# Moving the attention of groups five to eleven by a weight pair, holding their first scores, and chunking three more groups' Q and K

## The chip, the cores and the metric

The kernel runs on one NeuronCore of a Trainium2 chip. A core has a matrix engine (TensorE, PE in the profile, with weight loads shown apart as PEld), a vector engine (VectorE, DVE), a scalar engine (ScalarE, ACT), a general engine (GpSimd, POOL) and a queue engine (SyncE, SP) that here issues most DMA transfers. Each engine works through its own instruction stream in order, and they wait for each other by semaphores. The metric is the device time of one execution, in microseconds.

## The reference

Two layers, one behind the other. The first is a linear attention with a complex decay, for 4 batches, 8 heads, 768 steps and 48 channels a head:

```python
a_re_n, a_im_n = (a_re * scale, a_im * scale)      # scale = min(|a|, 0.999) / (|a| + 1e-6)
for t in range(S):
    S_re, S_im = ar * S_re - ai * S_im + k[t] v[t]^T, ar * S_im + ai * S_re
    y[:, :, t] = q[:, :, t] @ S_re
```

The second is a mixture of four dense experts on the 3072 rows of 384 that y makes:

```python
p = domain_probs / (domain_probs.sum(-1, keepdims=True) + 1e-09)
for e in range(E):
    out += p[:, e:e + 1] * (np.maximum(x @ w1[e], 0.0) @ w2[e])   # 384 -> 1024 -> 384
```

Everything is float32 in and out.

## The kernel before, in words

**Groups and blocks.** The 3072 rows are cut into twelve groups of 256 (three to a batch), each of two chunks of 128. While the attention of group g is computed, TensorE also does experts 0 and 1 for the rows of group g-1: that is block g-1. So block 4 carries the attention of group 5. After the last block a second phase does experts 2 and 3 for all rows.

**A block's dense part.** The weights of two experts lie in SBUF as sixteen tiles, taken two at a time: eight weight pairs, k = 0 to 7. For a pair, `w1_step` makes the first layer (tile `ph`, 18 matmuls, line 237: each weight and each x is split in a high and a low part, and three products are summed), ScalarE and VectorE make the hidden rows in high and low part (`hh` line 247, `hl` line 248), and `w2_step` adds the second layer to `po` (line 258, 12 matmuls). The second layer of a pair is emitted after the first layer of the next one.

**Attention of a group.** VectorE and ScalarE prepare it ahead, in `norm` (decays normalised), `prefix` (running products of decays, lines 423 to 426 and 366 to 374) and `finish`, whose head multiplies Q with them (line 494) and whose tail makes K (lines 509 to 513). Q and K are then in a layout with channels of all heads in the partitions. `trip` turns them to one head's channels in the partitions by writing them to DRAM (`q_d`, `k_d`, line 523) and reading them back (`Qst`, `Kst`, line 530). `attention` uses them in three pieces:

- the first: K of chunk 0 turned on TensorE (`ktp`, line 564), the state's increment (`dp`, line 583), and the first scores (`sc`, line 599, two halves of eight matmuls in all, masked on VectorE into `scs`, line 604);
- the second: values of chunk 0 (`yp`, lines 616 and 621), decay factors, scores of chunk 1;
- the third: values of chunk 1, y to DRAM (`y_d`, line 699) and back as the block's next input (`xa`, line 217), the turn and increment of chunk 1, and the state's rotation (lines 639 to 642, not for the last group of a batch; nor are its turn and increment of chunk 1).

The input is split in high and low part (`xha` line 224 on ScalarE, `xla` line 226 on VectorE), emitted ahead of pair 7 and needed at the next block's first pair.

**Where the pieces stand.** `between(k)` is called ahead of each pair of a block. From `FIRST[g]` on (2 where it has no entry) it emits one piece of group g's attention at each of three calls, so the third piece stands ahead of pair `FIRST[g]` + 2. At each call it also advances the preparation of the next group, by a budget in microseconds (`STEP`, `MORE`). One point of that stream is held: the tail of group g+1, which writes K, is emitted only after the third piece of group g's attention (`over`).

**HALF.** For the groups in `HALF`, Q and K make the trip one chunk at a time, and the tail computes K one chunk at a time, chunk 0 first; the others send both chunks in one transfer for each of the real and the imaginary part. After a group's trips stands a tiny DMA that reads `Kst` (line 873), and behind it on SP the loads of the next group's Q and K and of the decays after that.

**Order.** The emission gives the order by which a planner arranges the instructions: it simulates the engines with its own costs and moves instructions ahead of others on the same engine when it believes them ready. `behind(ins, prev)` forbids one such move: `ins` may not be placed ahead of `prev` on the engine, without a wait of its own. The planner's clock is not the chip's, so an instruction can be placed where the chip does not have its data yet.

Of the kernel before, what the change touches and what calls it, by code (L numbers as in the profile page):

```python
# [55 lines left out]
WARM = {6: "pq", 7: "tk"}  # L56
NSEL = 2
XSEL = 3
FIRST = {1: 5, 2: 5, 3: 4, 4: 4, 5: 3, 6: 3}
STEP = {1: 4.2, 2: 4.2, 3: 4.2, 4: 4.2, 5: 4.2}  # L60
MORE = (1.9, 1.9, 0.5)
HALF = (2, 3, 4, 5)
HOFF = 96
WIDE = 32 + P + 48
DMA_SCRATCH = 4096
# [56 lines left out]
def fast_path(ctx, tc, qkP, aP, vP, probsP, w, out, flag):  # L122
# [41 lines left out]
    wts = {}  # L164
    whi = {}

    def behind(ins, prev):
        tc.add_manual_dep(ins.ins, prev.ins.name,
                          mybir.DependencyInfo(mybir.DependencyClass.NoSync, mybir.DependencyReason.DATA),
                          reason="issue order")  # L170
# [44 lines left out]
    def load_x(g):  # L215
        x = moe.tile([P, NJ, G], F32, tag="x", name=f"xa{g}", bufs=1)
        nc.sync.dma_start(x, y_d[g].rearrange("(j p) t -> p j t", p=P))
        return [(slice(0, G), x)]
# [11 lines left out]
    def w1_step(b, xh, xl, f2, prev=None):  # L230
        ph = ps_h.tile([P, 2, G], F32, tag="ph", name=f"ph{b}_{f2}")
        for u in range(2):
            hi, lo = wts[2 * f2 + u]
            n = 0
            for wt, xt in ((hi, xh), (lo, xh), (hi, xl)):
                for j in range(NJ):
                    ins = nc.tensor.matmul(ph[:, u, :], wt[:, j * P:(j + 1) * P], xt[:, j, :],  # L237
                                           start=(n == 0), stop=(n == 3 * NJ - 1))
                    if u == 1 and n == 0:
                        wts["w1"] = ins  # L240
                        tc.keep_in_program_order(ins)
                    elif n == 0 and prev is not None:
                        behind(ins, prev)
                    n += 1
        hh = moe.tile([P, 2, G], F32R, tag="hh", name=f"hh{b}_{f2}")
        hl = moe.tile([P, 2, G], F32R, tag="hl", name=f"hl{b}_{f2}")
        wts["hh"] = nc.scalar.activation(hh, ph, AF.Relu)  # L247
        nc.vector.scalar_tensor_tensor(hl, ph, 0.0, hh, op0=ALU.max, op1=ALU.subtract)  # L248
        return hh, hl
# [16 lines left out]
    class MoE:  # L266
# [8 lines left out]
        def block(self, b, xh, xl, f_lo, f_hi, done, between=None, prev=None):  # L275
            po = None
            for f2 in range(f_lo // 2, f_hi // 2):
                if between is not None:
                    between(f2 - f_lo // 2)
                hh, hl = w1_step(b, xh, xl, f2, prev if f2 == f_lo // 2 else None)  # L280
                self.flush()
                if (2 * f2) % FE == 0:
                    po = [ps_o.tile([P, HD], F32, tag="po", name=f"po{b}_{f2}_{t}") for t in range(CG)]

                def fin(f2=f2, hh=hh, hl=hl, po=po):
                    w2_step(f2, hh, hl, po, wts.pop(("hold", b, f2), ()))
                    if (2 * f2 + 2) % FE == 0:
                        done(2 * f2 // FE, po)
                self.pend = fin
# [3 lines left out]
    with ExitStack() as c1:  # L293
# [225 lines left out]
        def trip(nm, X, dst, lo=0, hi=CG, prev=None):  # L519
            w = X.shape[-1] if hi == CG else C  # L520
            dt = dram.tile([2, HD, hi - lo, w], F32, name=nm)
            for c in range(2):
                sent = nc.sync.dma_start(dt[c].rearrange("(j p) n t -> p j n t", p=P),
                                         X[:, c].rearrange("p (j n) t -> p j n t", n=CG)[:, :, lo:hi, :w])
                if prev is not None:
                    behind(sent, prev)

            def back(prev=None):
                for c in range(2):
                    landed = nc.sync.dma_start(dst[c * IM:c * IM + D, :, lo:hi, :w],  # L530
                                               dt[c].rearrange("(h d) n t -> d h n t", d=D))
                    if prev is not None:
                        behind(landed, prev)
                return landed
            back.sent = sent
            return back

        def t_factors(g):
            Tr, Ti = Qst[0:D, :, CG - 1, C:], Qst[IM:M, :, CG - 1, C:]
            ins = nc.scalar.activation(TA[0:D], Tr, AF.Copy)  # L540
            tc.keep_in_program_order(ins)
            behind(ins, state["y", g, CG - 1 if g < NSEL else 0])
            tc.keep_in_program_order(nc.scalar.activation(TA[IM:M], Tr, AF.Copy))
            tc.keep_in_program_order(nc.scalar.activation(TB[IM:M], Ti, AF.Copy))
            tc.keep_in_program_order(nc.scalar.activation(TB[0:D], Ti, AF.Copy, scale=-1.0))
# [85 lines left out]
        def rotate(g):  # L631
            if (g + 1) % GB == 0:
                return
            Gt = state[g, CG]

            def bt(ap):
                return ap.broadcast_to([ap.shape[0], H, D])

            nc.vector.tensor_tensor(P2[0:D], Gt[IM:M], bt(TB[IM:M]), op=ALU.mult)
            nc.vector.tensor_tensor(P2[IM:M], Gt[0:D], bt(TB[0:D]), op=ALU.mult)  # L640
            nc.vector.tensor_tensor(Gt, Gt, bt(TA), op=ALU.mult)
            state["dve"] = nc.vector.tensor_tensor(Gt, Gt, P2, op=ALU.add)
            state[g + 1, 0] = Gt

        def turn_x(g, c, y):
            xp = ps_a.tile([P, NJ, C], F32, tag="pa", name=f"xp{g}_{c}")
            for j in range(NJ):
                ps = [p for p in range(HP) if -HOFF < 2 * D * p - P * j < P]
                for p in ps:
                    o = HOFF - (2 * D * p - P * j)  # L650
                    ins = nc.tensor.matmul(xp[:, j, :], band[:, o:o + P], y[:, p, c * C:(c + 1) * C],
                                           start=(p == ps[0]), stop=(p == ps[-1]))
                    if g == 0 and c == 0 and p == ps[0]:
                        behind(ins, state["yl", g, 1])
            last["xp"] = ins
            return slice(c * C, (c + 1) * C), xp
# [39 lines left out]
        def store_y(g, y):  # L696
            yv = y_d[g].rearrange("(p u d) t -> u d p t", u=2, d=D)
            for u in range(2):
                nc.sync.dma_start(yv[u], y[u * IM:u * IM + D])

        def attention(g, QK):
            y = small.tile([M, HP, G], F32, tag="y", name=f"y{g}")
            (turn0, _, inc0, sc0, val0), (turn1, _, inc1, sc1, val1) = (chunk(g, c, QK[1], y) for c in range(CG))
            turn0()
            inc0()
            yield sc0()
            val0()
            t_factors(g)
            sc1()
            xs = [turn_x(g, 0, y)] if g < XSEL else None  # L710
            if g < XSEL:
                wts["hold", g - 1, NF1 // 2 - 2] = ((5, state["sc", g, 1]),)
            yield
            val1()
            if g < XSEL:
                xs.append(turn_x(g, 1, y))
                wts["hold", g - 1, NF1 // 2 - 1] = ((0, state["yl", g, 1]), (8, last["xp"]))
            store_y(g, y)
            x = xs or load_x(g)
            turn1()  # L720
            inc1()
            rotate(g)
            yield x
# [67 lines left out]
        def front(g, A, qk):  # L791
# [36 lines left out]
            yield 3.0  # L828
            if g in HALF:
                qb = [trip(f"q_d{g}_{c}", Q, Qst, c, c + 1) for c in range(CG)]  # L830
# [10 lines left out]
            else:  # L841
# [5 lines left out]
                qb()  # L847
                last["q"] = kb()
            todo[g] = attention(g, (Q, K))

        x = {}
# [54 lines left out]
        for g in range(1, NG + 1):  # L906
            if g == NG:
                check_all()
                for e, h in late_d:
                    late_weights(e, h)  # L910
            first = FIRST.get(g, 2)
            end = first + len(MORE) - 1
# [586 lines left out]
```

## Time and profile before

| what | value |
|---|---|
| timed runs | 981.01, 984.24, 989.49 us; median 984.24 |
| the profiled execution | 989.45 us, its span 987.6 us |
| granted TensorE clock, mean | 0.988 of full |
| ScalarE, GpSimd busy | 479.6 us (49%), 165.9 us (17%) |
| DMA | 139.60 MB, mean 141 GB/s |

The profile is one execution. Its page gives busy times, the chain of work that ended last and the costliest groups of instructions; the trace behind it also answers which engine waited for what, in any stretch of time, and lists instructions in order. Lines such as L599 are lines of the kernel, and a name such as `Kst<-k_d` is what an instruction writes and what it reads. Matmuls are pipelined, so a busy TensorE is not always one at its peak. The blocks of attention last from about 51 to 614 us, the second phase from there to the end. Block 4 begins at about 238 us, and blocks 4 to 10, in which groups 5 to 11 have their attention, end at about 573 us.

### The profile page before, as it was taken

How to read it: one execution, taken by the hardware profiler on the slowest of the kernel's cores; microseconds unless marked ns; L12 is line 12 of the kernel's file. 1: busy time of each engine (PE TensorE's matmuls, PEld its weight loads, DVE VectorE, ACT ScalarE, POOL GpSimd, SP SyncE). 2: the span in 40 equal slices, each digit the busy share in tenths (PEclk: the TensorE clock that was granted, in tenths of full speed). 3: DMA queues.
4: the chain of work that ended last, by engine and by line, in shares of the span. 5: the costliest groups of instructions: out<-in, count | busy, mean ns of one | idle time of the engine just before them, and what ended most of it. 6: DMA issues, size and time to landing. Idle time of an engine off the chain costs nothing.

```text
span 987.6 us, 18277 instructions
## 1 busy us (share of the span) xinstructions
PE 952.5 (96%) x7037; PEld 920.5 (93%) x7037; DVE 739.5 (75%) x1610; ACT 479.6 (49%) x952; POOL 165.9 (17%) x206
## 2 busy tenths in 40 slices
PE   5899999999998999999999999999999999999997
PEld 2799999999898989899998999999999999999997
DVE  7889989898787989788887556767575848576643
ACT  7755536354353626264444345645554545454430
POOL 6030000000000000000000006533443342323000
PEclk9899999999899999999999999999999999999999
DMA  9585277582837556483939759421513453231112
GB/s 309 171 163 151 73 177 155 143 194 88 200 96 177 129 153 168 105 192 113 217 90 290 279 167 329 103 97 48 129 55 114 157 138 90 75 97 49 49 49 76
DMA packets 112258, 139.60 MB, mean 141 GB/s; under 512 B 8034, under 2 KB 95890, under 8 KB 112162
## 3 DMA queue, kind: packets, MB, share of 16 engines
q1 hardware_dynamic: 100674, 111.42, 39.7%
q0 software_dynamic: 11488, 26.93, 11.7%
q8 instruction: 57, 0.93, 0.4%
q14 instruction: 39, 0.32, 0.1%
HBM read 89.82 MB, written 48.49 MB: 140 GB/s over the span
## 4 chain that ended last, share of the span: by engine, by line
PE 75%; DMA 12%; DVE 6%; ACT 3%; issue 1%; SPq 0%; DVEq 0%; ACTq 0%
PE pob L961 20%; PE pb L961 17%; PE ph L237 13%; PE po L258 13%; PE sc L599 5%; DMA Kst<-k_d 4%; DMA k_d<-K 4%; PE yp L621 2%; PE yp L616 2%; DMA q_d<-Q 2%; PE dp L583 1%; DVE K L513 1%; DMA y_d<-y 1%; PE ktp L564 1%; DVE Q L494 1%
## 5 line engine op out<-in xcount | busy, mean ns | idle before, releaser
L961 PE MATMUL pob<-shi,hid 128*128 128x384 f32 x528 | 148.4, 334 | 0.0
L258 PE MATMUL po<-whi,hh 128*128 128x384 f32 x384 | 130.5, 340 | 0.0
L258 PE MATMUL po<-wlo,hh 128*128 128x384 f32 x384 | 129.3, 337 | 0.0
L247 ACT ACTIVATE hh<-ph 128x512 fp32r<-128x512 f32 x96 | 57.2, 596 | 111.9 <-PE ph L237 102.9
L973 POOL TENSOR_TENSOR Z<-Z 128x384 f32<-128x384 f32 x84 | 90.7, 1125 | 111.0 <-DMA Z<-y_d 56.2
L237 PE MATMUL ph<-xha,whi 128*128 128x256 f32 x576 | 104.0, 287 | 1.2 <-ACT xha L224 1.2
L237 PE MATMUL ph<-xha,wlo 128*128 128x256 f32 x576 | 102.8, 284 | 0.0
L237 PE MATMUL ph<-xla,whi 128*128 128x256 f32 x576 | 101.6, 284 | 0.6 <-DVE xla L226 0.6
L961 PE MATMUL pb<-xh,shi 128*128 128x384 f32 x291 | 97.2, 335 | 0.6 <-DVE pb L967 0.6
L961 PEld LDWEIGHTS pob<-shi,hid 128*128 128x128 f32 x528 | 96.4, 188 | 0.2 <-DVE hid L970 0.2
L961 PE MATMUL pb<-xh,slo 128*128 128x384 f32 x288 | 96.2, 334 | 0.0
L961 PE MATMUL pb<-xl,shi 128*128 128x384 f32 x288 | 96.2, 334 | 0.0
L248 DVE SCALAR_TENSOR_TENSOR hl<-ph,hh 128x512 fp32r<-128x512 f32 x96 | 65.9, 687 | 38.7 <-ACT hh L247 38.1
L237 PEld LDWEIGHTS ph<-xha,whi 128*128 128x128 f32 x576 | 86.0, 190 | 2.9 <-ACT xha L224 1.7
L961 PE MATMUL pob<-slo,hid 128*128 128x384 f32 x264 | 88.2, 334 | 0.0
L258 PE MATMUL po<-whi,hl 128*128 128x384 f32 x384 | 86.4, 338 | 0.0
L237 PEld LDWEIGHTS ph<-xla,whi 128*128 128x128 f32 x576 | 82.9, 191 | 1.2 <-DVE xla L226 0.8
L237 PEld LDWEIGHTS ph<-xha,wlo 128*128 128x128 f32 x576 | 83.1, 190 | 0.4 <-issue 0.2
L964 ACT ACTIVATE SN<-pb 128x384 f32<-128x384 f32 x96 | 47.3, 492 | 66.6 <-PE pb L961 59.2
L967 DVE TENSOR_TENSOR xl<-Z,xh 128x384 fp32r<-128x384 f32 x104 | 59.8, 606 | 21.1 <-ACT xh L964 10.9
L258 PEld LDWEIGHTS po<-whi,hh 128*128 128x128 f32 x384 | 72.7, 189 | 0.8 <-ACT acc L729 0.2
L258 PEld LDWEIGHTS po<-wlo,hh 128*128 128x128 f32 x384 | 72.8, 190 | 0.0
(227 smaller groups left out, 2050.6 us busy)
## 6 DMA issues: line engine op xcount, KB each, us to landing
qk<-qkP SPq DMA_DIRECT2D x24, 384.0 KB, 5.7
acc_d<-acc POOLq DMA_DIRECT2D x24, 384.0 KB, 5.2
ACC<-acc_d SPq DMA_DIRECT2D x48, 192.0 KB, 3.6
A<-aP SPq DMA_DIRECT2D x22, 384.0 KB, 6.8
Z<-y_d SPq DMA_DIRECT2D x16, 384.0 KB, 3.6
q_d<-Q SPq DMA_DIRECT2D x12, 387.0 KB, 5.0
Qst<-q_d SPq DMA_DIRECT2D x12, 387.0 KB, 5.9
v<-vP SPq DMA_DIRECT2D x24, 192.0 KB, 2.4
```

The source lines that it names most:

```text
L237: ins = nc.tensor.matmul(ph[:, u, :], wt[:, j * P:(j + 1) * P], xt[:, j, :], start=(n == 0), stop=(n == 3 * NJ - 1))
L247: wts["hh"] = nc.scalar.activation(hh, ph, AF.Relu)
L248: nc.vector.scalar_tensor_tensor(hl, ph, 0.0, hh, op0=ALU.max, op1=ALU.subtract)
L258: ins = nc.tensor.matmul(po[t], part[0][:, u, t * P:(t + 1) * P], wts[i][n][:, HD:], start=(i % FE == 0 and part[0] is hh and n == 0), sto ...
L494: ins = nc.vector.tensor_tensor(dst(Q[:, c, :, :C], lo, hi), rows(A[:, c], lo, hi), rows(qk[:, 0], lo, hi), op=ALU.mult)
L599: ins = nc.tensor.matmul(s_ps[:, h, :], Kc[:, hf * 4 + h, :], Qc[:, hf * 4 + h, :], start=True, stop=True)
L616: ins = nc.tensor.matmul(yo, st[:, o:o + n], Qc[:, o // D, :], start=True, stop=False)
L621: ins = nc.tensor.matmul(yo, vc[:, o:o + n], sc[h // 4][:, h % 4, :], start=first, stop=True)
L961: return tc.keep_in_program_order(nc.tensor.matmul(*args, **kw))
L964: return pin(nc.scalar.activation(dst, src, fn, scale=scale))
L967: pin(nc.vector.tensor_tensor(dst, x, y, op=op))
L973: nc.gpsimd.tensor_tensor(dst, x, y, op=op)
```

## The change

Three edits.

- `FIRST` is raised: groups 5 and 6 from 3 to 4, group 7 from 2 to 4, groups 8 to 11 from 2 to 3. All three pieces move together, and with the third piece the point after which the next group's tail is emitted.
- The first scores (both halves of chunk 0) of groups from `NPIN` = 5 on are placed behind the last first-layer matmul that was emitted before them, that of pair `FIRST[g]` - 1. The planner could move them ahead of it until now.
- Groups 6, 7 and 8 join `HALF`.

```diff
-FIRST = {1: 5, 2: 5, 3: 4, 4: 4, 5: 3, 6: 3}
+NPIN = 5
+FIRST = {1: 5, 2: 5, 3: 4, 4: 4, 5: 4, 6: 4, 7: 4, 8: 3, 9: 3, 10: 3, 11: 3}
...
-HALF = (2, 3, 4, 5)
+HALF = (2, 3, 4, 5, 6, 7, 8)
...
                     n += 1
+        wts["w1e"] = ins
         hh = moe.tile([P, 2, G], F32R, tag="hh", name=f"hh{b}_{f2}")
...
             turn0()
             inc0()
-            yield sc0()
+            yield sc0(prev=wts["w1e"] if g >= NPIN else None)
             val0()
```

## The prediction

> **What bounds the kernel now.** I read the page's busy line and chain first, then TensorE's waits (over the span and block by block), then the granted clock by stretch, and last the chain and timelines around groups five, six and seven.
>
> ```profile
> PE 952.5 (96%) x7037; PEld 920.5 (93%) x7037; DVE 739.5 (75%) x1610; ACT 479.6 (49%) x952; POOL 165.9 (17%) x206
> PE 75%; DMA 12%; DVE 6%; ACT 3%; issue 1%; SPq 0%; DVEq 0%; ACTq 0%
> ```
>
> TensorE is busy 96% of the 987.6 us span, yet only 75% of the chain that ended last is TensorE, and 12% is DMA. So some work comes just late, off TensorE. TensorE's waits (engine, line, what ended the wait: total, times, longest) show what:
>
> ```profile
> PE sc L599 <- DMA Kst<-k_d: 11.5, 7, 3.4
> ```
>
> Most of what TensorE waits for in the middle of the kernel is the first scores of a group, for K on its way back from DRAM. The same question put to stretches of about one block each gives, for groups 5, 6, 7, 8, 10 and 11 in this order (group 9 has no such wait):
>
> ```profile
> PE sc L599 <- DMA Kst<-k_d: 2.4, 1, 2.4
> PE sc L599 <- DMA Kst<-k_d: 3.4, 1, 3.4
> PE sc L599 <- DMA Kst<-k_d: 1.3, 1, 1.3
> PE sc L599 <- DMA Kst<-k_d: 1.1, 1, 1.1
> PE sc L599 <- DMA Kst<-k_d: 0.7, 1, 0.7
> PE sc L599 <- DMA Kst<-k_d: 2.1, 1, 2.1
> ```
>
> Sum: 2.4 + 3.4 + 1.3 + 1.1 + 0.7 + 2.1 = 11.0 us, all in groups that the change moves. Now the clock, by stretch (start:end, length, busy us of PE, PEld, DVE, ACT and POOL, granted clock, DMA share, GB/s):
>
> ```profile
> 261.50:268.40 6.90, 6.58 (x50) 6.29 (x51) 2.86 (x8) 0.00 (x0) 0.00 (x0) 0.51 1.12 281
> 312.70:316.10 3.40, 3.40 (x18) 3.40 (x18) 1.20 (x3) 0.00 (x0) 0.00 (x0) 0.51 0.91 355
> 316.10:541.40 225.30, 220.19 (x1928) 209.97 (x1927) 191.06 (x433) 108.22 (x202) 7.15 (x10) 1.00 0.61 158
> 541.40:544.90 3.50, 3.50 (x17) 3.50 (x18) 3.09 (x7) 0.63 (x1) 0.00 (x0) 0.51 1.07 292
> ```
>
> After each of the three waits over 2 us (groups 5, 6, 11) the clock is granted at half for 6.9, 3.4 and 3.5 us; between 316 and 541 us, where the waits are 1.3 us or less, it stays at 1.00. Half clock costs half of those stretches: 0.49 x 13.8 = 6.8 us.
>
> What the change can win in this execution is thus 11.0 + 6.8 = 17.8 us. Three blocks, each read from the second pair's start to the next block's second pair, bear it out:
>
> ```profile
> 242.30:292.30 50.00, 47.53 (x376) 45.42 (x376) 39.43 (x91) 22.15 (x42) 1.43 (x2) 0.93 0.55 135
> 292.30:342.80 50.50, 47.14 (x398) 45.06 (x398) 42.02 (x88) 27.90 (x50) 1.44 (x2) 0.97 0.61 159
> 435.90:481.10 45.20, 45.20 (x398) 43.45 (x397) 38.54 (x84) 23.08 (x43) 1.44 (x2) 1.00 0.59 151
> ```
>
> The block from 435.9 has no wait, TensorE is full, and it lasts 45.2 us; those from 242.3 and 292.3 last 50.0 and 50.5. VectorE needs 38.5 to 42 us of a block of 45: it has room, but only some 3 to 7 us, which matters below.
>
> **Part by part.** *Scores later and held.* A weight pair is one 18-matmul first layer (ph) and one 12-matmul second layer (po):
>
> ```profile
> 338.69 2.15 PE ph L237 x18
> 340.84 2.08 PE po L258 x12
> 312.49 3.53 PE sc L599 x16
> 316.02 0.21 PE ph L237
> 316.24 2.11 PE po L258 x12
> ```
>
> One pair is 2.15 + 2.08 = 4.23 us. What counts is not the move in the emission but how much TensorE work that now stands behind the first scores comes ahead of them. The hold forbids scores before the last first-layer matmul of pair FIRST - 1. For group 6 (the last three rows, in the chain's order) the scores now sit one ph short of a pair's first layer; they go behind that ph and, I expect, the twelve po: 0.21 + 2.11 = 2.3 us against a 3.4 us wait. Group 7, moved by two pairs, and 8 to 11 get between half a pair and a whole one, 2.1 to 4.2 us, against 1.3, 1.1, none, 0.7 and 2.1: covered. Group 5 is different; its scores were late already:
>
> ```profile
> 261.82 0.77 PE sc L599 x2
> 262.59 1.67 PE dp L583 x26
> 264.26 3.29 PE sc L599 x14
> 267.55 1.65 PE po L258 x7
> ```
>
> They stand behind pair 3's first layer, which is just what the hold asks, so only the seven po move ahead (7 x 2.08/12 = 1.2 us at full clock), and perhaps the increment (26 dp, half of 1.67, 0.8 us at full clock). That leaves 2.4 - 1.2 - 0.8 = 0.4, to 1.2 us; I take 0.7. At 1.3 us and less the clock held, by the rows above.
>
> *Q and K by chunk for six to eight.* The DMA issues (out<-in, count, KB each, median us to landing), then the VectorE forms of the K product (count, busy, mean ns, idle before):
>
> ```profile
> k_d<-K SPq DMA_DIRECT2D x12, 384.0 KB, 6.6
> Kst<-k_d SPq DMA_DIRECT2D x12, 384.0 KB, 5.5
> k_d<-K SPq DMA_DIRECT2D x16, 192.0 KB, 3.9
> Kst<-k_d SPq DMA_DIRECT2D x16, 192.0 KB, 5.1
> L513 DVE TENSOR_TENSOR K<-A,u 128x384 f32<-128x384 f32 x24 | 12.1, 550 | 0.1
> L513 DVE TENSOR_TENSOR K<-A,u 128x768 f32<-128x768 f32 x12 | 10.9, 952 | 0.0
> ```
>
> The first chunk's trip is 3.9 + 5.1 = 9.0 us instead of 6.6 + 5.5 = 12.1: 3.1 us earlier, for groups 6 to 8. Against it stand ten half-size VectorE operations for five whole ones, 10 x 0.55 - 5 x 0.95 = 0.75 us a group at most, and eight more DMA issues a group on SP, queued ahead of the next Q/K and A loads, which have most of a block to land. I cost both at nothing: VectorE's 3 to 7 us and SP's idle time hide them; uncovered, the VectorE part is 3 x 0.75 = 2.3 us.
>
> *What is late next: the next block's input.* A group's third piece stores y, reloads it as x and splits it, due when the next block starts; for group 5 it moves one pair nearer to that start. The chain there today, the first matmul of the next block, and two jobs that group 6 has behind its third piece:
>
> ```profile
> 280.21 0.61 ACT y L627
> 280.83 4.57 DMA y_d<-y
> 285.46 2.97 DMA xa<-y_d
> 288.45 0.85 ACT xha L224
> 289.33 0.96 DVE xla L226
> 290.29 0.47 DVE s L489
> 292.29 0.52 PE L237 MATMUL ph<-xha,whi 128*128 128x256 f32 x3
> 327.80 0.81 PE ktp L564 x6
> 333.12 0.95 PE dp L583 x27
> ```
>
> From the start of y's last copy (280.21) to the end of xha (289.30) it is 9.1 us, and the block starts 12.1 us after that copy: 3.0 us to spare. One pair takes 4.23 of it, so x(5) is late by 1.2 us, bounded by 0 (if a second layer is put first) and 3 (a slower DMA). I take 1.4. Groups 6 and 7 also end at pair 6, but have a turn and an increment behind the third piece, 0.81 + 0.95 = 1.8 us more cover: on time. Groups 8 to 11 end at pair 5 and keep a pair.
>
> The row of s L489 shows the other side: VectorE's head work for K(6) stands behind xla(5) today. With x(5) later and the head emitted before it, I expect that order to turn and K(6) to come sooner; if not, K(6) moves with x(5), and group 6 keeps up to 2 us of its wait. I take 0.7.
>
> **Sum.** The profiled execution took 989.45 us (span 987.6). 989.45 - 17.8 + 0.7 (scores of 5) + 1.4 (x of 5) + 0.7 (scores of 6) = 974.5. The three timed runs (981.01 to 989.49, median 984.24) reach below that execution; I read this as fewer or shorter waits of this kind in them, which lowers what can be won there but not the floor of 989.45 - 17.8 = 971.7. Against the median, 974.5 is -1.0%.
>
> **Rivals.** *K moves along (0.22).* The stream emits the next group's K only after this group's third piece, so K(6) to K(11) may come as many pairs later as the scores. For it: the order of emission. Against it: around 290 us the work ahead of K is the chain of x quoted above, not an emission. Then the waits stay, less what the chunks' 3.1 us take: 3.1 + 1.3 + 1.1 and group 6's half clock, 1.7, together 7.2. With 1.4 for x(5): 989.45 - 7.2 + 1.4 = 983.7, the median's level.
>
> *The half clock stays (0.06).* If the three stretches at 0.51 had another cause than the waits before them, only group 6's, behind the longest, would go: 989.45 - 11.0 - 1.7 + 2.8 = 979.6. Against it: each starts as such a wait ends, and between 316 and 541 us there is none. [...]
>
> *The x load takes the place (0.12, slower).* The starts of blocks 5, 6 and 7 wait for x instead. The cover from y's last copy to the next start becomes 12.1 - 4.2 = 7.9 us for group 5 and 9.7 for 6 and 7. If store and load meet the stream's transfers and take what K's whole ones take (6.6 + 5.5, with 0.6 of copy and 0.85 of split 13.6), x is late by 5.7 + 3.9 + 3.9 = 13.5 us, and the clock halves after each (three times 1.7 to 3.4, say 8): 989.45 - 17.8 + 13.5 + 8 + 1.4 = 994.5. It decides from a chain of about 11.7 us, where all three waits pass 2 us and the clock begins to fall (971.7 + 1.4 + 7.8 + 5.1 = 986); today's rows show 9.1, which speaks against it.
>
> *More than counted (0.04).* Below 969, if VectorE, no longer held behind late scores, also closed small gaps elsewhere; no row promises it.
>
> **Numbers.** The forecast case has 0.56, with its own range of 970 to 979. With the second and third cases the range is 969 to 986. About 1% is what a measurement of this kernel can tell from no change: 974.4 and 994.1. Rather over half of the forecast case lies below 974.4, since the waits added are taken high and the runs' spread comes mostly from waits that go; with the last case 0.38 faster. The rest of it, the second and third cases and a part of the fourth make 0.52 the same; 0.10 slower.
>
> **What would show it.** Right: no wait of the first scores for Kst over about 1 us in groups 5 to 11, no half clock between 240 and 600 us, blocks of 44 to 47 us there, a small wait of ph for xha or xla near 288 us. Wrong: waits of scores that stay though their place among the pairs moved (the second case), waits of ph for xha or xla over 3 us at several block starts (the fourth), or half clock without a wait before it (the third).

## The result and the profile after

The changed kernel takes 974.76 us in the median of five runs (973.38 to 975.42), the kernel before beside it 985.34 (981.01 to 989.49): a ratio of 0.9908, interval 0.9881 to 0.9935. (Ratios here are estimates over the runs side by side; the quotient of the two medians is 0.9893.) The forecast was 974.5. The profiled execution took 974.37 us (span 972.7) against 989.45 before: 15.1 us less.

The page of the changed kernel, its busy line, the granted clock in 40 slices and the chain that ended last:

```profile
PE 945.0 (97%) x7037; PEld 913.5 (94%) x7037; DVE 740.7 (76%) x1625; ACT 480.1 (49%) x952; POOL 165.6 (17%) x206
...
PEclk9999999999999999999999999999999999999999
...
PE 84%; DVE 5%; DMA 4%; ACT 2%; issue 1%; SPq 0%; POOL 0%; DVEq 0%; ACTq 0%
```

DMA's share of the chain falls from 12% to 4%, TensorE's rises from 75% to 84%. TensorE's busy time falls by 7.5 us with the same 7037 matmuls. At half clock matmuls last longer and count as busy for longer (before, group 11's first scores took 421 ns each at a granted clock of 0.51, group 9's 275 ns at 1.00, in the median); the forecast's 6.8 us of half clock are most of this. TensorE's waits from 235 to 562 us (engine, line, what ended the wait: total, times, longest) are now these:

```profile
PE sc L601 <- DMA Kst<-k_d: 1.5, 1, 1.5
PE sc L601 <- issue: 1.0, 1, 1.0
PE yp L623 <- DVE scs L606: 0.2, 1, 0.2
PE po L260 <- ACT acc L731: 0.2, 1, 0.2
```

The first is group 11's, the second group 9's; groups 5, 6, 7, 8 and 10 have none. (For some waits no releaser is found and the view says "issue"; group 9's stands where a wait for `Kst` would.) The 11.0 us of before are 2.5.

The seven blocks that carry groups 5 to 11, cut at the same matmuls as before (start:end, length, busy us of PE, PEld, DVE, ACT and POOL, granted clock, DMA share, GB/s):

```profile
242.10:286.80 44.70, 44.53 (x376) 42.55 (x376) 41.27 (x95) 24.13 (x45) 1.43 (x2) 1.00 0.65 163
286.80:331.70 44.90, 44.90 (x398) 43.35 (x398) 38.34 (x87) 23.86 (x44) 1.44 (x2) 1.00 0.67 154
331.70:380.80 49.10, 49.10 (x433) 46.89 (x432) 44.71 (x100) 25.41 (x47) 1.43 (x2) 1.00 0.65 157
380.80:422.10 41.30, 41.30 (x356) 40.02 (x355) 34.79 (x78) 19.75 (x35) 1.43 (x2) 1.00 0.57 149
...
sum 319.40, PE 316.52 PEld 302.74 DVE 267.98 ACT 153.88 POOL 10.02; mean PE 45.22 PEld 43.25 DVE 38.28 ACT 21.98 POOL 1.43
```

The sum of the same view of before:

```profile
sum 334.50, PE 323.56 PEld 309.37 DVE 266.57 ACT 153.44 POOL 10.02; mean PE 46.22 PEld 44.20 DVE 38.08 ACT 21.92 POOL 1.43
```

334.5 - 319.4 = 15.1 us: all of the gain lies in these blocks. The first two fall from 50.0 and 50.5 to 44.7 and 44.9, the length that the undisturbed block of before had (45.2). Single blocks aren't comparable further than that, because some work moved from one to the next (433 matmuls in the third against 414 before, 356 in the fourth against 375); the sums are comparable.

### The profile page after: what moved, and what is told of

Same layout as the page of the kernel before. It is cut to its first block, busy times and chain, and to the rows that moved or that the text cites. A ratio compares the mean times of both kernels' runs of the same rounds, so it can differ in the third digit from the quotient of the medians.

```text
span 972.7 us, 18333 instructions
## 1 busy us (share of the span) xinstructions
PE 945.0 (97%) x7037; PEld 913.5 (94%) x7037; DVE 740.7 (76%) x1625; ACT 480.1 (49%) x952; POOL 165.6 (17%) x206
## 4 chain that ended last, share of the span: by engine, by line
PE 84%; DVE 5%; DMA 4%; ACT 2%; issue 1%; SPq 0%; POOL 0%; DVEq 0%; ACTq 0%
PE pob L963 20%; PE ph L238 18%; PE po L260 17%; PE pb L963 17%; PE sc L601 4%; PE yp L623 2%; PE dp L585 2%; PE yp L618 2%; PE ktp L566 1%; DMA lw<-w 1%; DMA shi<-w 1%; PE xp L653 1%; DMA Kst<-k_d 1%; DVE Q L496 1%; DMA q_d<-Q 1%
## 5 line engine op out<-in xcount | busy, mean ns | idle before, releaser
L966 ACT ACTIVATE hid<-pb 128x384 fp32r<-128x384 f32 x76 | 37.3, 490 | 71.9 <-PE pb L963 71.4
```

What stands on the lines that cost most here:

```text
L966: return pin(nc.scalar.activation(dst, src, fn, scale=scale))
```

## The experiments

Each diff says which kernel it starts from. Line numbers are those of the changed kernel, two higher than before. `NPIN`, and the line that notes the last first-layer matmul, do nothing by themselves.

**The parts alone.** Four kernels compared on one chip with the kernel before (983.55 us in the median of 29 runs). First, only `FIRST`; against the changed kernel:

```diff
-HALF = (2, 3, 4, 5, 6, 7, 8)
+HALF = (2, 3, 4, 5)
...
-            yield sc0(prev=wts["w1e"] if g >= NPIN else None)
+            yield sc0()
```

> Only FIRST is raised; no hold, groups 6 to 8 whole. In the order of the program the first scores of groups 5, 6, 7, 9, 10 and 11 stand exactly where they stand in the changed kernel; only group 8's are put earlier, ahead of its pair 2's second-layer work (58 first and 56 second layers done, against 59 and 58). My theory (what counts is the TensorE work between K's store and the first scores): waits of 5, 7 and 10 gone, 6 keeps 0 to 1 us, 9 and 11 keep 1 to 1.5 us, and group 8 waits 4 to 6 us and brings back half clock (1.7 to 3.4 us): 981 to 986 us. Rival 'K moves along': waits of 1 to 3 us in all of groups 6 to 11, 984 or more. Rival 'chunks carry the gain': as before, 985.

981.23 us (977.92 to 986.14), ratio 0.9977 (0.9954 to 1.0). The waits of scores fall, but not to nothing, and a wait at the start of block 7 comes in, for x (view of waits, 238 to 575 us):

```profile
PE sc L601 <- DMA Kst<-k_d: 3.0, 2, 1.6
PE ph L238 <- ACT xha L225: 2.5, 1, 2.5
```

Group 8 doesn't wait for K at all. I had put 4 to 6 us on it; this was wrong. Its scores come 11.1 us after K's last operation (381.7 us): beside one and a quarter weight pairs, TensorE has group 8's own turn and increment to do in between, and stands still for 2.5 us, the wait for x.

Second, `FIRST` and the hold; against the changed kernel:

```diff
-HALF = (2, 3, 4, 5, 6, 7, 8)
+HALF = (2, 3, 4, 5)
```

> FIRST and the hold, groups 6 to 8 whole; the first scores of all groups stand where the changed kernel has them. My theory: the waits go without the chunks too, group 6 to 8 keep at most 1 us together, no half clock: 975 to 977 us. Rival 'chunks carry the gain': waits in 6, 7 and 8 of 1 to 3 us come back, 980 to 984. Rival 'K moves along': 984.

979.46 us (976.8 to 980.91), ratio 0.9955 (0.9936 to 0.9975). The waits are much the same: 2.6 and 1.0 us for scores, 1.5 for x. The 975 to 977 us that I expected were too few. The profiled execution took 976.8 us, the shortest of the twelve, and has no half clock between 240 and 600 us (mean granted clock 0.998 over the whole span); what the others lose beside it is not in this profile.

Third, only `HALF`; against the kernel before:

```diff
-HALF = (2, 3, 4, 5)
+HALF = (2, 3, 4, 5, 6, 7, 8)
```

> Only groups 6 to 8 by chunk, FIRST as before (with it the hold changes no instruction's place, so that part alone is the kernel before). My theory: group 6's 3.4 us wait falls to 0 to 1 with its half clock, 7 and 8 lose their 1.1 to 1.3, but group 5's 2.4 with 3.4 us of half clock and group 11's 2.1 with 1.7 stay: 978 to 981 us. Rival 'chunks carry the gain': 975 to 976.

980.08 us (976.98 to 985.07), ratio 0.9953 (0.993 to 0.9975). Group 5, which this part doesn't touch, still waits 2.1 us (the row for `Qst`), with a half clock of 3.4 us behind it (granted clock 0.50 from 260.70 to 264.11 us), and of the groups it does touch, 8 has no wait, 6 waits 0.65 us. Group 7 waits more than before, 2.0 instead of 1.3 us (the row "issue"): its K came earlier and the planner moved its scores earlier still, to 49.9 weight pairs from the start of block 0 instead of 50.6.

```profile
PE sc L601 <- DMA Kst<-k_d: 2.9, 3, 1.2
PE sc L601 <- DMA Qst<-q_d: 2.1, 1, 2.1
PE sc L601 <- issue: 2.0, 1, 2.0
```

Fourth, everything but the hold; against the changed kernel:

```diff
-            yield sc0(prev=wts["w1e"] if g >= NPIN else None)
+            yield sc0()
```

> FIRST and the chunks without the hold; again only group 8's first scores stand earlier (58 and 56 layers done). My theory: K's first chunk is there 3 us sooner than whole K, so group 8 waits 0 to 3 us: 975 to 979 us, and what this and the run without chunks differ by is group 8's wait and its half clock. Rival 'K moves along': 980 or more.

974.77 us (973.79 to 977.57), ratio 0.9902 (0.9874 to 0.993): as fast as the whole change. The profiled execution, the longest of the six, has waits of 0.7 us in group 9 and 2.3 in group 11, with 3.4 us at half clock behind the second (mean granted clock 0.995 over the span). Group 8, which I gave up to 3 us, has none.

So the two parts, `FIRST` with the hold and the chunks, are worth about half a per cent each (0.9955 and 0.9953). Together they agree with what they give one by one: 0.9955 x 0.9953 = 0.9908, the ratio measured. The intervals, 0.002 to either side, are too wide to show that the parts simply add. The hold adds nothing that these runs can tell (0.9908 with it and 0.9902 without; without the chunks 0.9955 and 0.9977, whose intervals overlap). It also does little to the order. Put alone into the kernel before, or alone with the chunks, it leaves the order of the instructions on every engine of the built program as it was; with `FIRST` raised, the scores of group 8 alone stand elsewhere in the planned order, one and a half pairs later. The planner would have placed all others as late by itself.

**Which groups' moves count.** Three kernels on one chip (before: 981.6 us, 14 runs). Groups 8 to 11 are left where they were:

```diff
-FIRST = {1: 5, 2: 5, 3: 4, 4: 4, 5: 4, 6: 4, 7: 4, 8: 3, 9: 3, 10: 3, 11: 3}
+FIRST = {1: 5, 2: 5, 3: 4, 4: 4, 5: 4, 6: 4, 7: 4}
```

> The changed kernel, but groups 8 to 11 keep the old place (FIRST 2); 5 to 7 stay moved, chunks and hold stay. First scores of 8 to 11 then stand at 58, 66, 74 and 82 first layers, one less than in the changed kernel. My theory (the place of the scores decides): group 10's 0.7 and group 11's 2.1 with half clock of 1.7 come back and 9's 1.0 and 11's 1.5 go, net 1.5 to 3 us: 976 to 978 us. Rival 'K moved along in 9 and 11, so their move won nothing': 974 to 975, with the same or smaller waits.

972.78 us (972.33 to 973.25), ratio 0.9905 (0.9877 to 0.9933), where I had expected 976 to 978. The move of groups 8 to 11 wins nothing that these runs can tell (0.9905 without it, 0.9908 with it): without it there is one wait left of scores, group 10's, and none in 9 and 11.

```profile
PE sc L601 <- DMA Kst<-k_d: 1.4, 1, 1.4
```

One half of why is seen in the TensorE work that lies between K and the first scores. In the kernel before, from the end of K's last operation to the first scores of groups 9 and 11, the first-layer matmuls (start:end, length, PE busy and count, clock, DMA share, GB/s), and then the second-layer ones:

```profile
433.52:447.37 13.85, 6.44 (x50) 1.00 0.96 209
524.62:541.33 16.71, 6.46 (x51) 1.00 1.07 307
...
433.52:447.37 13.85, 6.83 (x36) 1.00 0.96 209
524.62:541.33 16.71, 7.56 (x36) 1.00 1.07 307
```

The same two views of the changed kernel:

```profile
424.15:437.97 13.82, 5.14 (x39) 1.00 0.90 169
517.15:531.29 14.14, 5.81 (x46) 1.00 0.98 274
...
424.15:437.97 13.82, 6.99 (x36) 1.00 0.90 169
517.15:531.29 14.14, 5.76 (x28) 1.00 0.98 274
```

The scores moved by a pair, but K moved by more. By matmuls at the prediction's durations (2.15 us for 18, 2.08 us for 12) group 9 has 11 first-layer matmuls less ahead of its scores, 1.3 us, and group 11 five and eight less, 0.6 + 1.4 = 2.0 us. In group 9 a wait of 1.0 us came up where there was none; in group 11 K was back after 14.14 us instead of 16.71, which made up for the 2.0 us, and 1.5 of 2.1 us of wait stayed.

The other half is K's way through DRAM, which doesn't take the same time in every kernel. With groups 8 to 11 left alone, group 11 has K and scores at the same pairs as in the kernel before, and yet no wait, because K is back within 15.2 us instead of 16.7. Group 9 has still less work behind K there than in the changed kernel (the same two views of that run), and doesn't wait either:

```profile
421.19:431.93 10.74, 4.63 (x36) 1.00 0.93 207
421.19:431.93 10.74, 4.85 (x24) 1.00 0.93 207
```

The DMA issues of K(9) in the changed kernel, and with groups 8 to 11 left alone (out<-in, count, KB each, median us to landing):

```profile
Kst<-k_d SPq DMA_DIRECT2D x2, 384.0 KB, 7.7
k_d<-K SPq DMA_DIRECT2D x1, 384.0 KB, 6.0
...
Kst<-k_d SPq DMA_DIRECT2D x2, 384.0 KB, 5.2
k_d<-K SPq DMA_DIRECT2D x1, 384.0 KB, 4.3
```

From the end of K's last operation to the landing this makes 13.7 us in the one and 9.5 in the other. It is 13.3 to 13.7 us in all five profiles in which groups 8 to 11 have their new place and K(9) goes whole, 11.5 to 11.7 in three in which at most group 5 has moved, and 9.0 to 9.5 in two in which groups 5 to 7 have. Beside the kernel before, group 9 thus lost 1.0 us of TensorE's work of all kinds ahead of its scores (13.9 to 12.9 us) and 2.2 us on the way (11.5 to 13.7). What makes the way longer was not tried.

One pair later for all seven groups:

```diff
-FIRST = {1: 5, 2: 5, 3: 4, 4: 4, 5: 4, 6: 4, 7: 4, 8: 3, 9: 3, 10: 3, 11: 3}
+FIRST = {1: 5, 2: 5, 3: 4, 4: 4, 5: 5, 6: 5, 7: 5, 8: 4, 9: 4, 10: 4, 11: 4}
```

> The changed kernel with groups 5 to 11 one pair later still (FIRST 5 for 5 to 7, 4 for 8 to 11). My theory: the waits of the first scores are gone or stay only where K moves along, but the next block's x becomes late: its chain of 9 to 10 us has about 3.6 us of cover for group 5, 5.4 for 6 and 7 and 8 to 10 for 8 to 11; the planner fills some 2 to 4 us of each with second layers. Waits of ph for xha or xla of 1 to 4 us at the starts of blocks 5 to 7, 3 to 8 us in sum, with half clock: 978 to 985 us. Rival 'the later the better': 972 to 974.

991.93 us (991.14 to 992.83), ratio 1.0101 (1.0072 to 1.013): slower than before, and slower than the 978 to 985 that I gave it. No scores wait; the blocks' first layers wait for x instead:

```profile
PE ph L238 <- ACT xha L225: 10.6, 4, 4.6
PE ph L238 <- DVE xla L227: 1.6, 1, 1.6
```

10.6 + 1.6 + two smaller waits of 0.9 and 0.4 = 13.5 us of waits, and 17.1 us at half clock (6.83 + 3.41 + 6.83, granted clock 0.50 in the second of them and 0.987 in the mean over the span; 2.2 of them are idle, and by my estimate the rest costs half, 7.4), less the 2.9 us of waits of the changed kernel: +18.0. Its span is 990.7, 18.0 above 972.7. This is the prediction's rival "the x load takes the place", one pair further on.

By chunk in groups 9 to 11 too:

```diff
-HALF = (2, 3, 4, 5, 6, 7, 8)
+HALF = (2, 3, 4, 5, 6, 7, 8, 9, 10, 11)
```

> The changed kernel with groups 9, 10 and 11 by chunk too. What is left of waits in the changed kernel is 1.0 us at group 9's first scores and 1.5 us at group 11's. My theory: both go, since the first chunk's trip is 3 us shorter: 972 to 973.5 us. Rival 'they wait for something else than the trip' (the loads of late weights on the same queue, or the planner moving K later): no change, 974.5 to 976.

975.74 us (974.97 to 977.08), ratio 0.9943 (0.9922 to 0.9964); I had expected 972 to 973.5. The waits of scores are gone, and others have come in blocks 10 and 11, for the masked scores, for x and for `hl`, so that nothing is won:

```profile
PE yp L623 <- DVE scs L606: 1.2, 2, 1.0
PE ph L238 <- ACT xha L225: 1.1, 1, 1.1
PE po L260 <- DVE hl L250: 0.9, 1, 0.9
```

Two of the three are VectorE's, whose operations on K have twice the count and over half the length each (in the changed kernel 0.55 us on one chunk, 0.95 us on both). That this load is what makes them late was not tried by itself.

**Group 5 alone, and a repair.** On one chip (before: 981.0 us, 22 runs), beside the changed kernel once more:

> The changed kernel once more, as the measure for the two others on the same chip: 973.5 to 975.5 us, waits of about 1.0 us at group 9's and 1.5 us at group 11's first scores.

972.8 us (971.78 to 976.1), ratio 0.9916 (0.9886 to 0.9945).

Of the moves, only group 5's, with the chunks; against the changed kernel:

```diff
-FIRST = {1: 5, 2: 5, 3: 4, 4: 4, 5: 4, 6: 4, 7: 4, 8: 3, 9: 3, 10: 3, 11: 3}
+FIRST = {1: 5, 2: 5, 3: 4, 4: 4, 5: 4, 6: 3}
```

> Groups 6 to 8 by chunk, and of the moves group 5's alone (FIRST 5: 4, the rest as before). Against chunks alone, whose profile had waits of 2.1 (group 5, with 1.7 of half clock), 0.7, 2.0, none, none, 1.1 and 1.2: my theory takes away group 5's 2.1 and its half clock, about 3.8 us of 980.1 over the runs before on their chip: 976 to 977.5 us, with waits of 1 to 2 us kept at groups 7, 10 and 11. Rival 'group 5's move frees VectorE ahead of K(6) and all later waits go': 973 to 974.5.

973.59 us (972.52 to 975.79), ratio 0.9925 (0.9901 to 0.9948). Moving one group of the seven gives what moving all gives, within the intervals. (The interval also overlaps that of the chunks alone, 0.993 to 0.9975, so group 5's share is not measured closely.) I had reckoned 976 to 977.5 us on the chip on which the parts were run, where the kernel before took 983.55; as a ratio that is 0.992 to 0.994, and it fits. Its profile has 1.7 us of wait in group 7 (shown as "issue"), 1.0 in 11 and 0.2 in 6, and 3.4 us at half clock behind the first (granted clock 0.50 from 345.48 to 348.89 us), which another execution may not have (see the last section). The two long ones:

```profile
PE sc L601 <- issue: 1.7, 1, 1.7
PE sc L601 <- DMA lw<-w: 1.0, 1, 1.0
```

And the repair of the kernel that leaves groups 8 to 11 alone: its one wait is group 10's, so group 10 goes by chunk.

```diff
-FIRST = {1: 5, 2: 5, 3: 4, 4: 4, 5: 4, 6: 4, 7: 4, 8: 3, 9: 3, 10: 3, 11: 3}
+FIRST = {1: 5, 2: 5, 3: 4, 4: 4, 5: 4, 6: 4, 7: 4}
...
-HALF = (2, 3, 4, 5, 6, 7, 8)
+HALF = (2, 3, 4, 5, 6, 7, 8, 10)
```

> Groups 5 to 7 moved, 8 to 11 at the old place (FIRST 2), and group 10 by chunk beside 6 to 8. The one wait of the first scores that was left with groups 8 to 11 at the old place is group 10's, 1.4 us; its first chunk comes some 2 to 3 us sooner. My theory: that wait goes, 1 to 1.5 us under the run without group 10's chunks, 971 to 972 us, and 2 to 3.5 us under the changed kernel on this chip. Rival 'the planner takes back what it is given' (it puts the scores earlier or K later, as it did for group 7 when only chunks were added): no change, 972.5 to 974.

976.78 us (972.81 to 978.33), ratio 0.9958 (0.9938 to 0.9978), against 971 to 972 expected, and above the 972.5 to 974 of the rival too. Group 10's wait is gone and group 11 waits 3.1 us, with 6.8 us at half clock behind it (mean granted clock 0.996 over the span):

```profile
PE sc L601 <- DMA Kst<-k_d: 3.1, 1, 3.1
```

Its last operation on K(11) stands at 79.4 pairs from the start of block 0; without group 10's chunks it was 78.5. The scores stayed at 81.5. So the wait was passed on to the next group. Why K(11) came a pair later was not found out.

No version beats the change beyond its interval; 0.9905 with groups 8 to 11 left alone is the same with a smaller edit.

## Why the prediction was right, point by point

**The size.** 974.5 was forecast against 974.76, and against the profiled execution 974.5 against 974.37. "Within 1%" had 0.52 and 0.9908 falls there, but the interval reaches over the border, so the runs don't settle on which side of it the change lies. The sum is right with other small terms than the forecast's. Of the signs it named, there is no half clock, but group 11 waits 1.5 us, two blocks last 41.3 and 49.1 us instead of 44 to 47, and the small wait for x near 288 us isn't there.

**The half clock, 6.8 us: right.** It is gone between 240 and 600 us (granted clock 1.00 in each of the seven blocks), so the rival "the half clock stays" is out. That only group 6's stretch would go (3.4 us, counted at 1.7), as that rival had it, no run shows: in the changed kernel's profile all three are gone. It is no sure gain in each execution, though: another profiled execution of the changed kernel has one stretch of 3.4 us (last section).

**The waits of groups 5 to 8, 8.2 us: right.** None is left. As far as the intervals tell, the move of group 5 with the chunks takes nearly all of the gain.

**Scores of 5, +0.7 expected: 0.** The chain of before had the scores right behind pair 3's first layer, and I let only seven po move ahead, since the hold asks no more. The planner put the scores behind pair 4's first layer, a whole pair. The hold is a lower bound, the planner's place is not.

**x of 5, +1.4 expected: 0.** The chain from y's last copy to the end of `xha`, which the forecast took over as 9.1 us, was shorter. On ScalarE in the changed kernel:

```profile
278.94 0.59 ACT L629 ACTIVATE y<-yp 48x512 f32<-48x512 f32 x1
285.80 0.83 ACT L225 ACTIVATE xha<-xa 128x768 fp32r<-128x768 f32 x1
```

That is 7.7 us, inside the 7.85 us to the block's first matmul; y's store took 2.9 us of it instead of 4.6. The chain is 7.7 to 7.9 us in all nine profiles in which group 5 has its new place, and 9.1 and 9.8 in the two in which it has the old one; why, was not found out. `xla` is done at 287.95, over a microsecond after the block's start. The timeline of TensorE there:

```profile
286.79 0.52 PE L238 MATMUL ph<-xha,whi 128*128 128x256 f32 x3
287.15 0.52 PE L238 MATMUL ph<-xha,wlo 128*128 128x256 f32 x3
287.51 0.34 PE L260 MATMUL po<-whi,hh 128*128 128x384 f32 x1
287.68 0.34 PE L260 MATMUL po<-wlo,hh 128*128 128x384 f32 x1
```

After the six matmuls that need only `xha`, the planner put second-layer matmuls in front of those that need `xla`, which start at 288.93. So the forecast's lower bound of 0 came true, but the second layer that it named for it ("if a second layer is put first") covers `xla` only; `xha` was in time because its chain was short.

**Order of VectorE: right.** Before, `xla` (289.33) stood ahead of the head's s (290.29); now, on VectorE:

```profile
282.09 0.56 DVE L491 CUSTOM_DVE_ANT_1 s<-s 128x384 f32<-128x384 f32 x1
287.00 0.95 DVE L227 TENSOR_TENSOR xla<-xa,xha 128x768 fp32r<-128x768 f32 x1
289.41 1.02 DVE L515 TENSOR_TENSOR K<-A,u 128x384 f32<-128x384 f32 x2
```

The head comes first, and K(6)'s first chunk is done at 290.4 us, 15 us ahead of its scores at 305.6; the 0.7 us left to **scores of 6** was 0.

**K moves along (0.22, all groups): wrong as a whole, right in two.** Against the kernel with only the chunks, the last operation on K stands 0.3 pairs earlier in group 6 and 0.5 later in 7 and 8, while the first scores move by 0.6, 1.6 and 1.0 pairs; in 10 it stays. K(9) and K(11) move by 1.0 and 1.4, their scores by 0.7 and 1.0, and the forecast, which called 8 to 11 covered by "half a pair and a whole one", had nothing for that. This is the step that failed: it counted the pairs by which the scores move and took K's place, and the time of its way through DRAM, for fixed. It left waits of 1.0 + 1.5 = 2.5 us where the forecast had none, and these happen to stand for the 2.8 us of the three terms above that weren't there: 17.8 - 2.5 = 15.3, against 15.1.

**The chunks' costs at nothing: right.** DVE's busy time rose by 1.2 us in all (739.5 to 740.7), less than the 2.3 that I gave for it uncovered, and no wait of TensorE in groups 6 to 8 came with it. What the chunks are for shows in the kernel that has only `FIRST`: its 1.6 us wait of group 7's scores and its 2.5 us for x at block 7's start are not there in the changed kernel, nor in the one that differs from it by the chunks alone.

**The x load takes the place (0.12): not here, but next.** It comes one pair later, with the waits and half clocks that make that version 1% slower. The forecast's 3.0 us to spare would not have paid for the first pair of 4.23; the shorter chain did. For the second pair nothing is left: group 5's chain takes 9.8 us there and TensorE waits 3.6 us for it.

## What to carry to other kernels

A wait for data that comes back by DMA is taken away (here 8.2 us, in groups 5 to 8) by putting more of the busy engine's work between the producer and the consumer, so count that work in the new order, not the distance by which the consumer moved: the producer may be emitted behind something that moves too. And measure the data's way again in the new order: for the same K(9) it took 9.0 to 13.7 us here. Test such a move group by group, since here one of seven came, with the chunks, within the intervals of all seven, four gave nothing that could be told, and one step more made the kernel slower than it had been. And take a planner's place for an instruction, not a lower bound put on it, as its place.

## What the runs showed of the hardware

Some waits of about 2 us were followed by half clock and others were not. In the kernel before, waits of 2.4, 3.4 and 2.1 us had 6.83, 3.41 and 3.41 us at half clock behind them. From the kernel with only the chunks, two waits of about the same length (2.1 and 2.0 us), in rows of 3.41 us, the length of the half clock behind the first (start:end, length, PE busy and count, clock, DMA share, GB/s):

```profile
257.29:260.70 3.41, 1.30 (x9) 1.00 1.08 223
260.70:264.11 3.41, 3.41 (x39) 0.50 1.18 238
346.03:349.44 3.41, 2.93 (x47) 1.00 1.14 230
349.44:352.85 3.41, 1.89 (x17) 1.00 1.24 174
352.85:356.26 3.41, 3.41 (x24) 1.00 1.11 261
```

Behind the first wait the granted clock is 0.50 for 3.41 us; the row ahead of that has 1.30 us of work and 2.11 without. Behind the second it stays at 1.00; the two rows in which this wait falls have 0.48 and 1.52 us without work.

In the kernel with only `FIRST`, a wait of 1.6 us, group 7's, had half clock behind it (granted clock 0.50 from 352.35 to 355.76 us), which by half of its length cost another 1.7 us, an estimate. The wait of 2.5 us at block 7's start had none (1.00 from 379.66 to 389.90 us). So in these runs the length of a wait doesn't tell by itself what follows it.

It also differs between two executions of one kernel. The two profiled ones of the changed kernel have 1.53 us without work in the one row and 1.94 in the other, both in group 11, with the clock at 1.00 behind the first and at 0.50 behind the second:

```profile
529.05:532.46 3.41, 1.88 (x33) 1.00 1.05 349
532.46:535.88 3.42, 3.42 (x30) 1.00 0.76 292
```

```profile
527.80:531.21 3.41, 1.47 (x30) 1.00 1.00 356
531.21:534.62 3.41, 3.41 (x19) 0.50 0.48 185
```

What decides whether half clock follows a wait was not shown: no run changed a wait and nothing else.
